# Packing the softmax row sums of eight heads, spreading their reciprocal by DMA, and running attention further ahead of an FFN

## The chip, the cores and the metric

The kernel runs on one core of one Trainium2 chip. The metric is the time of one execution on the device in microseconds (us). A single-core program can be compared run with run. All timed runs quoted as medians here are in the fast state (two probes that ran once have an unknown state, and only the durations of single instructions are read from them).

Five engines matter: TensorE (PE, matmuls), VectorE (DVE), ScalarE (ACT), GpSimd (POOL) and SyncE (SP). SP does no arithmetic here; its instruction queue issues DMAs. POOL's queue issues the DMAs that load and convert q, k, v and the weights.

## The reference

Sliding-window attention with a linear bias (ALiBi), then a gated FFN over all tokens:

```python
# q, k, v: (8 batches, 8 heads, 576 tokens, 64)
scores = q @ k.T / 8 + slope[h] * -(i - j)      # where 0 <= i - j < 128, else -1e9
attn   = softmax(scores)
x      = (attn @ v)  as (8*576, 512) tokens
out    = (gelu(x @ w_gate) * (x @ w_val)) @ w_out    # 512 -> 1536 -> 512
```

## The kernel before

Tokens are processed in nine groups of 512 for the FFN, and in eight batches of 576 for attention. A *stage* of the main loop is one group: a gate phase (`gate_val`, twelve blocks of eight matmuls) and an output phase (`out_half`, eight halves of six matmuls). The attention of the next batch is interleaved with the output phase: scores, exponential on ACT, mask on DVE, then `values` for each of four pairs of heads.

```python
    def transposes_dma(b):                      # issued by SP: ten DMA transposes per batch
        for nm, dst, off in (("ksb", kT[b % 2], 64), ("qsb", qT[b % 2], 0)):
            for j in range(5):
                ...
                nc.sync.dma_start_transpose(out=dst[:, :, off + 128 * j:...], in_=slabs[nm, b][0:sz, j, :])

    def values(b, c):                           # c: a pair of heads, i: the head in it
        ...
        for what in (0, 1):                     # 0: values, 1: row sums, with `ones` as weights
            for j in range(5):
                ...
                        w = vb[...] if what == 0 else ones          # 128 x 64
                        nc.tensor.matmul(out=ps[64 * i:64 * i + 64, base + a:base + e],
                                         lhsT=w, rhs=P[:, i, col:col + e - a], ...)
        r = r_pool.tile([128, S], FP32, name="r")
        nc.vector.reciprocal(r[:, 0:QS], z[:, 0:QS])
        nc.vector.tensor_tensor(out=xT[:, c, t0:t0 + QS], in0=x[:, 0:QS], in1=r[:, 0:QS], op=ALU.mult)
        nc.vector.reciprocal(r[:, QS:S], y[:, 256:512])
        nc.vector.tensor_tensor(out=xT[:, c, t0 + QS:t0 + S], in0=y[:, 0:256], in1=r[:, QS:S], op=ALU.mult)

    for g in range(NG):                         # the stages
        b = g + 1
        if 1 < b < B:
            load_qk(b); load_v(b)
        for f in range(NF):
            gate_val(g, f)
            if b < B and f == 0:
                transposes_dma(b)
        if b < B:
            scores0(b, 0); scores1(b, 0); out_half(g, 0); scores2(b, 0); out_half(g, 1)
            scores1(b, 1); out_half(g, 2); scores2(b, 1); values(b, 0); out_half(g, 3)
            ...                                 # and so on to values(b, 3), out_half(g, 7)
```

With 64 columns of ones as weights, the sum of a row arrives already copied to the 64 partitions where its head's values lie, so that the product needs no rearranging. The price is that each sum is inverted 64 times over.

The softmax here doesn't subtract the row's maximum and nothing guards it: scores larger than these inputs give would overflow.

## Time and profile before

| | before |
|---|---|
| time, median | 460.14 us (459.24 to 460.41, three runs) |
| span of the profiled execution | 457.4 us |
| first gate block with all its data | 48.3 us |
| a stage with attention | 51 us (the first two), 47.5 us (the later ones) |
| a stage without attention (the last two) | 31.1 us |

The head of the profile's page, busy time of each engine:

```profile
span 457.4 us, 6209 instructions
PE 377.6 (83%) x2424; PEld 179.0 (39%) x2424; DVE 283.7 (62%) x332; ACT 173.0 (38%) x314; POOL 110.3 (24%) x138
...
PE 54%; DVE 38%; ACT 3%; POOL 2%; issue 2%; POOLq 0%
```

The last line is the chain of work that ended last, followed back from the end, as shares of the span by engine. No engine is busy all the time, so the average tells little; a stage has to be cut into its phases. Busy time of each engine in the gate phase and in the output phase of one stage (start and end in us, length, then busy us and number of instructions per engine, the granted PE clock; the two last columns, of the DMA engines, are not used here):

```profile
core 0: us, PE busy (x) PEld busy (x) DVE busy (x) ACT busy (x) POOL busy (x), PEclk, DMA share, GB/s
246.90:267.10 20.20, 20.18 (x95) 9.03 (x95) 9.67 (x13) 8.50 (x14) 5.95 (x8) 1.00 0.81 98
267.10:294.40 27.30, 20.49 (x188) 10.32 (x188) 23.84 (x26) 11.46 (x23) 6.64 (x8) 0.94 0.74 78
```

The gate phase is PE alone, 20.2 us without a gap. In the output phase DVE is busy for 23.8 of 27.3 us and PE for 20.5. The chain of waits inside that phase (start, length, what), followed back from the end, says which of the two decides:

```profile
280.50 2.08 DVE r L203
...
283.09 1.67 DVE r L206
...
291.80 2.08 DVE r L203
...
294.44 0.59 PE ps L219 x2
```

Half of the chain in these 27.3 us is reciprocals (13.3 us, seven of them). In the whole kernel they cost 124.7 us, by the groups of instructions (line, engine, operation, shapes, count, then busy us in all, mean ns of one, idle time ahead):

```profile
L203 DVE RECIPROCAL r<-ps 128x320 f32<-128x320 f32 x32 | 68.8, 2150 | 0.0
L206 DVE RECIPROCAL r<-ps 128x256 f32<-128x256 f32 x32 | 55.9, 1747 | 0.0
```

SP's own queue is nearly empty. In order of time, one stage:

```profile
272.17 19.79 SPq L241 DMA_DIRECT2D out_dram<-osb  x4
292.06 6.53 SPq L127 DMA_TRANSPOSE kT<-ksb  x5
298.64 7.27 SPq L127 DMA_TRANSPOSE qT<-qsb  x5
```

Four output stores, each issued when its data is ready, then ten transposes at 1.3 us apart.

### The profile page before, as it was taken

What the parts mean: (1) busy time and instruction counts of PE and PEld (TensorE: products, weight loads), DVE (VectorE), ACT (ScalarE), POOL (GpSimd) and SP (SyncE); (2) the same over time, 40 slices, a digit from 0 to 9 for tenths busy, and PEclk for the clock granted to TensorE, in tenths of its full rate; (3) what the DMA queues carried; (4) which work ended last, traced back from release to release, by engine and by line L of the source; (5) the groups of instructions that cost most, each with busy time, mean ns of one, the idle gap of its engine ahead of it and who ended that gap; (6) DMA issues with size and microseconds to landing.
All of it is one profiled execution on the core that took longest, in us unless ns stands there. A gap on an engine that the chain in (4) does not pass through costs nothing.

```text
span 457.4 us, 6209 instructions
## 1 busy us (share of the span) xinstructions
PE 377.6 (83%) x2424; PEld 179.0 (39%) x2424; DVE 283.7 (62%) x332; ACT 173.0 (38%) x314; POOL 110.3 (24%) x138
## 2 busy tenths in 40 slices
PE   0483799669995899689968997699949995999995
PEld 0352344424442344334434443344424452344442
DVE  0579436973499346974598449944995399541430
ACT  1641237223650337233633364236514560331321
POOL 8947429122403070123303150300000000000000
PEclk9996799869997899889997999899989998899999
DMA  9999999894919592095909290940124011001002
GB/s 96 110 203 154 180 155 170 92 122 70 90 47 90 112 96 55 26 126 75 104 37 131 60 125 24 125 78 1 47 69 82 0 47 47 0 0 74 19 2 92
DMA packets 157998, 36.99 MB, mean 81 GB/s; under 512 B 147728, under 2 KB 153360, under 8 KB 157968
## 3 DMA queue, kind: packets, MB, share of 16 engines
q0 software_dynamic: 118288, 18.88, 56.4%
q1 hardware_dynamic: 39680, 17.71, 16.3%
q8 instruction: 19, 0.31, 0.3%
q14 instruction: 11, 0.09, 0.1%
HBM read 37.75 MB, written 9.44 MB: 103 GB/s over the span
## 4 chain that ended last, share of the span: by engine, by line
PE 54%; DVE 38%; ACT 3%; POOL 2%; issue 2%; POOLq 0%
PE ps L219 41%; DVE r L203 15%; PE ps L234 11%; DVE r L206 10%; DVE P L145 6%; DVE xT L204 3%; ACT P L142 3%; PE ps L135 2%; DVE xT L207 2%; POOL qsb L81 1%; DVE osb L105 1%; POOL ksb L81 1%; ACT emask L264 1%; DVE qT L105 0%; DVE emask L267 0%
## 5 line engine op out<-in xcount | busy, mean ns | idle before, releaser
L224 DVE TENSOR_TENSOR hT<-ps,gelu 128x512 bf16<-128x512 f32 x108 | 74.7, 692 | 112.4 <-PE ps L219 105.3
L219 PE MATMUL ps<-xT,wg 128*128 128x512 bf16 x432 | 117.8, 393 | 23.8 <-DVE xT L207 13.0
L219 PE MATMUL ps<-xT,wv 128*128 128x512 bf16 x432 | 114.4, 388 | 0.0
L234 PE MATMUL ps<-wo,hT 128*128 128x512 bf16 x432 | 109.9, 398 | 1.7 <-ACT osb L107 1.7
L223 ACT ACTIVATE gelu<-ps 128x512 bf16<-128x512 f32 x108 | 64.0, 597 | 120.9 <-PE ps L219 120.8
L142 ACT ACTIVATE P<-ps 128x512 bf16<-128x512 f32 (+2 forms) x160 | 73.7, 542 | 21.6 <-PE ps L135 21.6
L219 PEld LDWEIGHTS <-wv 128*128 128x128 bf16 x432 | 42.9, 99 | 76.9 <-issue 28.3
L203 DVE RECIPROCAL r<-ps 128x320 f32<-128x320 f32 x32 | 68.8, 2150 | 0.0
L219 PEld LDWEIGHTS <-wg 128*128 128x128 bf16 x432 | 43.8, 102 | 58.2 <-issue 11.5
L145 DVE TENSOR_TENSOR P<-P,emask 128x1024 bf16<-128x1024 bf16 x64 | 45.5, 721 | 26.2 <-ACT P L142 26.1
L234 PEld LDWEIGHTS <-hT 128*128 128x128 bf16 x432 | 39.5, 101 | 54.2 <-issue 17.0
L90 POOL DMA_DIRECT2D vb<-in_v_dram x40 | 34.1, 869 | 92.9 <-PE ps L197 92.1
L206 DVE RECIPROCAL r<-ps 128x256 f32<-128x256 f32 x32 | 55.9, 1747 | 0.0
L197 PE MATMUL ps<-P,vb 128*64 128x128 bf16 (+2 forms) x384 | 26.1, 282 | 32.4 <-DVE P L145 32.4
L81 POOL DMA_DIRECT2D qsb<-in_q_dram x40 | 33.8, 870 | 71.3 <-DMA qT<-qsb 64.9
L107 ACT COPY osb<-ps 128x512 f32<-128x512 f32 x18 | 10.6, 586 | 99.6 <-PE ps L234 99.6
L81 POOL DMA_DIRECT2D ksb<-in_k_dram x40 | 33.8, 887 | 17.1 <-DMA wo<-in_moe_w_out_dram 10.2
L197 PEld LDWEIGHTS <-vb 128*64 128x64 bf16 x384 | 18.7, 127 | 40.2 <-issue 38.8
L135 PE MATMUL ps<-qT,kT 64*128 64x256 bf16 (+2 forms) x320 | 27.3, 272 | 5.8 <-DVE qT L105 5.6
L197 PE MATMUL ps<-P,ones 128*64 128x128 bf16 (+2 forms) x384 | 25.8, 278 | 0.3
L135 PEld LDWEIGHTS <-kT 64*128 64x128 bf16 x320 | 10.6, 98 | 28.7 <-issue 26.6
L197 PEld LDWEIGHTS <-ones 128*64 128x64 bf16 x384 | 20.1, 130 | 1.2 <-issue 1.1
(32 smaller groups left out, 92.9 us busy)
## 6 DMA issues: line engine op xcount, KB each, us to landing
out_dram<-osb SPq DMA_DIRECT2D x36, 256.0 KB, 2.0
qsb<-in_q_dram POOLq DMA_DIRECT2D x32, 128.0 KB, 4.3
ksb<-in_k_dram POOLq DMA_DIRECT2D x32, 128.0 KB, 4.5
vb<-in_v_dram POOLq DMA_DIRECT2D x32, 128.0 KB, 4.5
wg<-in_moe_w_gate_dram POOLq DMA_DIRECT2D x4, 384.0 KB, 10.7
wv<-in_moe_w_val_dram POOLq DMA_DIRECT2D x4, 384.0 KB, 11.9
wo<-in_moe_w_out_dram POOLq DMA_DIRECT2D x1, 1536.0 KB, 17.2
kT<-ksb SPq DMA_TRANSPOSE x35, 3.2
```

What stands on the lines that cost most here:

```text
L81: nc.gpsimd.dma_start(out=t[0:sz, j, :].rearrange("p (h d) -> p h d", h=H), in_=src[b][:, 128 * j:128 * j + sz, :].rearrange("h p d -> p h ...
L90: nc.gpsimd.dma_start(out=t[lo:128, j, :].rearrange("p (h d) -> p h d", h=H), in_=v[b][:, 128 * j - 64 + lo:128 * j + 64, :].rearrange("h ...
L135: nc.tensor.matmul(out=ps[:, col:col + NQ[j]], lhsT=kT[b % 2][lo:lo + 64, c, 128 * j:128 * j + 128], rhs=qT[b % 2][lo:lo + 64, c, Q0[j]:Q0 ...
L142: nc.scalar.activation(out=dst, in_=src, func=AF.Exp, scale=0.125)
L145: nc.vector.tensor_tensor(out=dst, in0=dst, in1=m, op=ALU.mult)
L197: nc.tensor.matmul(out=ps[64 * i:64 * i + 64, base + a:base + e], lhsT=w, rhs=P[:, i, col:col + e - a], start=first, stop=last, skip_group ...
L203: nc.vector.reciprocal(r[:, 0:QS], z[:, 0:QS])
L206: nc.vector.reciprocal(r[:, QS:S], y[:, 256:512])
L219: nc.tensor.matmul(out=ps, lhsT=w[:, c, 128 * f:128 * (f + 1)], rhs=xT[:, c, t0:t0 + 512], start=(c == 0), stop=(c == 3))
L223: nc.scalar.activation(out=gl, in_=pg, func=AF.Gelu)
L224: nc.vector.tensor_tensor(out=hid[g][:, f, :], in0=pv, in1=gl, op=ALU.mult)
L234: nc.tensor.matmul(out=po, lhsT=hid[g][:, f, 128 * t:128 * (t + 1)], rhs=wo[:, f, :], start=(f == 0), stop=(f == NF - 1))
```

## The change

The intent: DVE inverts each row sum 16 times over and not 64 times, a quarter of the reciprocals. All eight heads' sums of a batch are packed into 128 rows (16 equal rows per head), one pair of reciprocals serves the batch, and 32 small DMAs spread it to the 64 partitions of each head. The spreading takes time, so attention moves further ahead: the scores of batch g+2 run in the output phase of group g, and the values of batch g+1 in its gate phase, where DVE has room.

```diff
@@ the sums and their reciprocals, once per batch
+    def sums(b):
+        ps = [bank(), bank()]
+        for j in range(5):
+            for s, a, e, col in pieces(j):
+                for i in (0, 1):
+                    for c in range(4):
+                        nc.tensor.matmul(
+                            out=ps[s][32 * c:32 * c + 32, a - QS * s:e - QS * s],
+                            lhsT=ones[:, i, :],                 # 128 x 32, ones in half of the columns
+                            rhs=probs[b, c - c % 2][:, c % 2, i, col:col + e - a], ...)
+        r = r_pool.tile([128, S], FP32, name="r")
+        nc.vector.reciprocal(r[:, 0:QS], ps[0][:, 0:QS])
+        nc.vector.reciprocal(r[:, QS:S], ps[1][:, 0:S - QS])
+        rb = r_pool.tile([128, 4, S], FP32, name="rb")
+        recip[b] = rb
+        for c in range(4):
+            for i in (0, 1):
+                row = 32 * c + 16 * i
+                for m in range(4):
+                    lo = 64 * i + 16 * m
+                    nc.sync.dma_start(out=rb[lo:lo + 16, c, :], in_=r[row:row + 16, :])
@@ values: the ones matmuls and the reciprocals are gone
-        nc.vector.reciprocal(r[:, 0:QS], z[:, 0:QS])
...
+            nc.vector.tensor_tensor(
+                out=xT[:, c, b * S + lo:b * S + hi], in0=ps[s][:, 0:hi - lo],
+                in1=recip[b][:, c, lo:hi], op=ALU.mult)
@@ the start: both batches 0 and 1 get their scores before the first gate block
+    transposes_dma(1)
+    for st in scores(0): st()
+    sums(0)
+    ...                            # scores(1) in two halves, values(0, 0..3) between and after
+    sums(1)
@@ the stages
     for g in range(NG):
+        if g + 2 < B:
+            load_qk(g + 2)
+            transposes_dma(g + 2)
         for f in range(NF):
             gate_val(g, f)
+            if g + 1 < B and f in (4, 6, 8, 10):
+                values(g + 1, f // 2 - 2)
+        b = g + 2
         if b < B:
+            load_v(b)
+            for u, st in enumerate(scores(b)):
+                st()
+                if u < 7:
+                    out_half(g, u)
+            sums(b)
+            out_half(g, 7)
```

Cut from the diff: the pools (the q/k slab goes from two buffers to one, the probabilities from two to three, the reciprocals from two to one), the output copies of most groups go to DVE alone, and the loads of batch 1's q and k move ahead of the weights.

More of the change, by code (lines that the diff above doesn't have):

```diff
@@ L48 @@
     consts = ctx.enter_context(tc.tile_pool(name="consts", bufs=1))
-    slab = ctx.enter_context(tc.tile_pool(name="slab", bufs=2))
-    p_pool = ctx.enter_context(tc.tile_pool(name="pp", bufs=2))
-    r_pool = ctx.enter_context(tc.tile_pool(name="rp", bufs=2))
+    slab = ctx.enter_context(tc.tile_pool(name="slab", bufs=1))
+    p_pool = ctx.enter_context(tc.tile_pool(name="pp", bufs=3))
+    r_pool = ctx.enter_context(tc.tile_pool(name="rp", bufs=1))
     h_pool = ctx.enter_context(tc.tile_pool(name="hp", bufs=2))
@@ L65 @@
     ident = consts.tile([128, 128], BF16, name="ident")
-    ones = consts.tile([128, 64], BF16, name="ones")
+    ones = consts.tile([128, 2, 32], BF16, name="ones")
     emask = consts.tile([128, H, 256], BF16, name="emask")
@@ L177, in scores2, with pieces @@
         mask(P[:, :, 512:1088], emask2[:, 2 * c:2 * c + 2, :])
+    def pieces(j):
+        a, e = Q0[j], Q0[j] + NQ[j]
+        if a < QS:
+            yield 0, a, min(e, QS), PCOL[j]
+        if e > QS:
+            yield 1, max(a, QS), e, PCOL[j] + max(a, QS) - a
+    recip = {}
+    def sums(b):
[7 more added lines that the diff above has]
+                            lhsT=ones[:, i, :],
+                            rhs=probs[b, c - c % 2][:, c % 2, i, col:col + e - a],
+                            start=(i == 0 and j == 2 * s), stop=(i == 1 and j == 2 * s + 2),
+                            skip_group_check=True)
+        r = r_pool.tile([128, S], FP32, name="r")
[9 more added lines that the diff above has]
+                    nc.sync.dma_start(out=rb[lo:lo + 16, c, :], in_=r[row:row + 16, :])
@@ L179, in values @@
     def values(b, c):
         P = probs[b, c - c % 2][:, c % 2]
-        x, y, z = bank(), bank(), bank()
-        for what in (0, 1):
-            for j in range(5):
-                for (a, e, ps, base) in (
-                        (Q0[j], min(Q0[j] + NQ[j], QS), (x, z)[what], 0),
-                        (max(Q0[j], QS), Q0[j] + NQ[j], y, 256 * what - QS)):
-                    if e <= a:
-                        continue
-                    first = (j == 0) if ps is not y else (j == 2 and what == 0)
-                    last = (j == 2) if ps is not y else (j == 4 and what == 1)
-                    for i in (0, 1):
-                        col = PCOL[j] + a - Q0[j]
-                        w = (vb[b % 2][:, j, 64 * (2 * c + i):64 * (2 * c + i) + 64]
-                             if what == 0 else ones)
-                        nc.tensor.matmul(
-                            out=ps[64 * i:64 * i + 64, base + a:base + e],
-                            lhsT=w, rhs=P[:, i, col:col + e - a],
-                            start=first, stop=last, skip_group_check=True)
@@ L201, in values @@
-        r = r_pool.tile([128, S], FP32, name="r")
-        t0 = b * S
-        nc.vector.reciprocal(r[:, 0:QS], z[:, 0:QS])
-        nc.vector.tensor_tensor(out=xT[:, c, t0:t0 + QS], in0=x[:, 0:QS],
-                                in1=r[:, 0:QS], op=ALU.mult)
-        nc.vector.reciprocal(r[:, QS:S], y[:, 256:512])
-        nc.vector.tensor_tensor(out=xT[:, c, t0 + QS:t0 + S], in0=y[:, 0:256],
-                                in1=r[:, QS:S], op=ALU.mult)
+        ps = [bank(), bank()]
+        for j in range(5):
+            for s, a, e, col in pieces(j):
+                for i in (0, 1):
+                    h = 2 * c + i
+                    nc.tensor.matmul(
+                        out=ps[s][64 * i:64 * i + 64, a - QS * s:e - QS * s],
+                        lhsT=vb[b % 2][:, j, 64 * h:64 * h + 64],
+                        rhs=P[:, i, col:col + e - a],
+                        start=(j == 2 * s), stop=(j == 2 * s + 2), skip_group_check=True)
@@ L210 @@
+        for s, (lo, hi) in enumerate(((0, QS), (QS, S))):
+            nc.vector.tensor_tensor(
+                out=xT[:, c, b * S + lo:b * S + hi], in0=ps[s][:, 0:hi - lo],
+                in1=recip[b][:, c, lo:hi], op=ALU.mult)
     hid = {}
@@ L238, in out_half @@
             osb = o_pool.tile([128, DM], FP32, name="osb")
-            evac(osb, po)
+            if g < B - 2:
+                nc.vector.tensor_copy(out=osb, in_=po)
+            else:
+                evac(osb, po)
             r0 = 512 * g + 128 * t
@@ L260 @@
         nc.vector.memset(vb[i][0:64, 0, :], 0.0)
-    nc.vector.memset(ones, 1.0)
+    nc.vector.memset(ones, 0.0)
+    for i in range(2):
+        nc.vector.memset(ones[:, i, 16 * i:16 * i + 16], 1.0)
     for h in range(H):
@@ L269, with scores @@
     step = DFF // 4
+    load_qk(1)
     for s in range(4):
         load_w(step * s, step * (s + 1))
-    load_qk(1)
     load_v(1)
     nc.gpsimd.dma_start(out=wo, in_=moe_w_out.rearrange("(c p) f -> p c f", p=128))
-    for c in range(4):
-        if c % 2 == 0:
-            for m in (c, c + 1):
-                transposes(0, m)
-                transposes(0, 4 + m)
-            scores0(0, c)
-        scores1(0, c)
-        scores2(0, c)
-        if c:
-            values(0, c - 1)
-    values(0, 3)
+    def scores(b):
+        for c in range(4):
+            if c % 2 == 0:
+                yield lambda c=c: (scores0(b, c), scores1(b, c))
+            else:
+                yield lambda c=c: scores1(b, c)
+            yield lambda c=c: scores2(b, c)
+    for i in (0, 1, 2, 3):
+        transposes(0, i)
+        transposes(0, 4 + i)
+    transposes_dma(1)
+    for st in scores(0):
+        st()
+    sums(0)
+    first = list(scores(1))
+    for st in first[0:4]:
+        st()
+    for c in range(2):
+        values(0, c)
+    for st in first[4:8]:
+        st()
+    for c in range(2, 4):
+        values(0, c)
+    sums(1)
     for g in range(NG):
-        b = g + 1
-        if 1 < b < B:
-            load_qk(b)
-            load_v(b)
+        if g + 2 < B:
+            load_qk(g + 2)
+            transposes_dma(g + 2)
         for f in range(NF):
             gate_val(g, f)
-            if b < B and f == 0:
-                transposes_dma(b)
+            if g + 1 < B and f in (4, 6, 8, 10):
+                values(g + 1, f // 2 - 2)
+        b = g + 2
         if b < B:
-            scores0(b, 0)
-            scores1(b, 0)
-            out_half(g, 0)
-            scores2(b, 0)
-            out_half(g, 1)
-            scores1(b, 1)
-            out_half(g, 2)
-            scores2(b, 1)
-            values(b, 0)
-            out_half(g, 3)
-            scores0(b, 2)
-            scores1(b, 2)
-            out_half(g, 4)
-            scores2(b, 2)
-            values(b, 1)
-            scores1(b, 3)
-            out_half(g, 5)
-            scores2(b, 3)
-            values(b, 2)
-            out_half(g, 6)
-            values(b, 3)
+            load_v(b)
+            for u, st in enumerate(scores(b)):
+                st()
+                if u < 7:
+                    out_half(g, u)
+            sums(b)
             out_half(g, 7)
```

## The prediction

> **What bounds it now.** In steady state one stage takes 47.5 us (chain of waits: 246.9 to 294.4): a gate phase of 20.2 us, PE alone, and an attention-and-output phase of about 27.2 us. There the chain runs through DVE: per batch four pairs of reciprocals (2.08 + 1.68 us each, 15 us), muls 3.7 us, masks 5.8 us (64 of 721 ns over 8 batches), an output copy. In that phase (busy-time windows, 267.2 to 294.4) DVE is busy 23.8 us and PE 20.4; PE stands idle up to 3.8 us at once, waiting for a mask, and its clock then falls to half for about 3 us. First gate starts about 48 us.
>
> **What the change does.** Reciprocals per batch: 15.6 us -> one pair, 3.9 us (off DVE: 11.7 us). Muls (3.7 us) move under the gate phase, where DVE has room (12 x 0.69 + 3.7 = 12 of 23 us). Output copies all go to DVE: +1.3 us. Row sums: still 48 matmuls per batch, now in four column groups instead of two; before 4 x 0.56 us, now about 1.7 us (estimate). The Trainium skill, "TensorEngine Tiling (Array Packing)", Tiling Modes, gives four independent tiles for 128x32. Small gain. PE work alone would allow a stage of about 41 us (20.7 gate + 2.4 values + 10.4 output + 3.5 scores + 1.7 sums + 2 waiting for the last mask).
>
> **What it adds.** 32 DMAs per batch on SP's queue, between the reciprocals and the ten DMA transposes of the next batch. In the trace an SP copy issue takes 332 ns plus about 0.1 us to the next; a transpose issues every 1.3 us, whether 128 or 64 rows, so I expect no discount for small copies. 32 x 0.42 = 13.4 us, plus 13 us of transposes, plus 2.4 us to landing. [...]
>
> Counted from the end of the sums: reciprocals +3.2, copies +13.4, last store +0.4, transposes +13, landing +2.4 = 32 us. But PE finishes the last output half, gate phase and values after about 24.5 us, and the scores need all those transposes. So PE waits about 7 us, its clock halves, and the output phase (9.1 output + 3.5 scores + 2 cold clock + 2 last mask + 1.7 sums) takes about 18 us. Stage: about 50 us, six times, instead of the 47.5 to 51 of before: the DVE gain is turned into a wait for SP's queue.
>
> **Start.** Both transposes and copies run on saturated DMA (9 tenths until 90 us in the slices; transposes there landed after 7 to 11 us), the values of batch 0 wait for copies queued after transposes of batch 1. First gate at about 60 to 66 us instead of 48, but holding batch 1's scores; stage 0 ends about 110 to 117.
>
> **Sum.** 113 + 5 x 49.5 + 34.5 (stage 6, no scores) + 62.2 (two stages without attention, 31.1 each) + 4.8 + 2.7 (time over span) = 465 us. Range 435 to 484. Faster by over 2%: 0.30; within: 0.30; slower: 0.40.
>
> **What would show it.** Reciprocals: 16 instructions, some 31 us in all. SP timeline: 32 copies in about 13 us, then transposes. PE: idle before the first score of each stage, released by a qT transpose, about 7 us, with half clock after. Muls inside the gate phase without waiting.
>
> **What would make it wrong.** If a 16-row copy issues in under 0.2 us, transposes land before the gate phase ends, a stage is 41 to 44 us and the kernel 410 to 435. If copies land late (DMA contention), DVE blocks on the muls and it is slower than 480. The start is the other uncertain term (10 us either way).

## The result, and the profile after

The kernel takes 524.14 us (522.81 to 524.61, four runs), against 460.27 us (459.24 to 461.43, four runs). The ratio is 1.138, with a 95% interval of 1.135 to 1.142: slower by 14%. Ratios are computed as the mean time of one kernel's fast runs over that of the other's fast runs of the same rounds, so they are not quite the ratio of the medians quoted. From the head of the profile's page:

```profile
span 522.0 us, 6526 instructions
PE 365.5 (70%) x2384; PEld 164.8 (32%) x2424; DVE 197.8 (38%) x298; ACT 164.3 (31%) x300; POOL 110.3 (21%) x138
...
PE 46%; SPq 32%; DMA 10%; issue 5%; DVE 3%; POOL 2%; ACT 1%; DVEq 0%; POOLq 0%
```

The last line is again the chain that ended last. DVE lost 86 us of work, as intended, and fell from 38% of the chain to 3%. In its place stands SPq, the issuing queue of SP, with 32%; it did not appear in the chain before. One stage, from the busy times (columns as before; now in three stretches):

```profile
...
306.40:330.10 23.70, 23.59 (x143) 10.73 (x143) 12.45 (x20) 7.39 (x13) 0.00 (x0) 1.00 0.22 50
330.10:344.60 14.50, 0.00 (x0) 0.00 (x0) 1.42 (x3) 1.06 (x1) 0.00 (x0) 0.69 0.42 101
344.60:363.50 18.90, 16.65 (x134) 6.80 (x138) 9.28 (x12) 10.64 (x21) 12.58 (x15) 0.88 1.59 137
```

The gate phase with the values in it is full, as planned. The output phase has shrunk from 27.3 to 18.9 us, as planned. Between them lie 14.5 us in which PE does nothing, and the stage is 57.1 us long instead of 47.5. The waits tell what PE and DVE wait for (engine, line, releaser, us in all, times, longest):

```profile
PE ps L135 <- DMA qT<-qsb: 112.0, 7, 25.9
...
DVE xT L227 <- DMA rb<-r: 41.8, 19, 4.8
```

(Two lines of the list of waits.) The first scores of a stage wait for the last transposes of q: once at the start (25.9 us) and six times in the stages. The second line is DVE waiting for the copies themselves before it can multiply (`xT`); whether that costs time is taken up below. SP's queue in the same stage shows where those transposes were:

```profile
308.58 20.75 SPq L212 DMA_DIRECT2D rb<-r  x32
329.43 0.53 SPq L265 DMA_DIRECT2D out_dram<-osb  x1
330.07 6.46 SPq L127 DMA_TRANSPOSE kT<-ksb  x5
336.58 6.79 SPq L127 DMA_TRANSPOSE qT<-qsb  x5
```

The 32 copies are issued first, one every 0.65 us, and the transposes come after them, because that is their order in the program. The chain of this stage shows only the second half of this:

```profile
328.26 1.85 PE ps L240 x8
330.11 1.21 SPq L127
...
342.19 2.31 DMA qT<-qsb
...
344.64 0.82 PE ps L135 x8
```

Ahead of the transposes the chain goes on with PE and not with the copies. The gate phase ended at 330.11 and the copies and the store at 330.0, so two paths end together there, and the chain, which follows inferred releases, could go on with only one. In a later stage (420 to 444 us) it goes through the copies. Such a tie is a reason to read the queue itself, and to test.

The groups of the reciprocals, which answer to those of before:

```profile
L203 DVE RECIPROCAL r<-ps 128x320 f32<-128x320 f32 x8 | 17.3, 2157 | 5.7 <-PE ps L196 5.7
L204 DVE RECIPROCAL r<-ps 128x256 f32<-128x256 f32 x8 | 13.6, 1696 | 0.0
```

And the copies in the page's list of DMA issues (count, KB each, median us from issue to landing):

```profile
rb<-r SPq DMA_DIRECT2D x256, 36.0 KB, 2.0
```

The reciprocals fell from 124.7 to 30.9 us. The copies land 2.0 us after issue (median), so they are not slow as transfers.

### The profile page after: what moved, and what is told of

It is laid out like the page before. It is cut to its first block, busy times and chain, and to the rows that moved or that the text cites. A ratio compares the mean times of both kernels' runs of the same rounds, so it can differ in the third digit from the quotient of the medians.

```text
span 522.0 us, 6526 instructions
## 1 busy us (share of the span) xinstructions
PE 365.5 (70%) x2384; PEld 164.8 (32%) x2424; DVE 197.8 (38%) x298; ACT 164.3 (31%) x300; POOL 110.3 (21%) x138
## 3 DMA queue, kind: packets, MB, share of 16 engines
q1 hardware_dynamic: 47872, 27.16, 20.8%
## 4 chain that ended last, share of the span: by engine, by line
PE 46%; SPq 32%; DMA 10%; issue 5%; DVE 3%; POOL 2%; ACT 1%; DVEq 0%; POOLq 0%
PE ps L240 20%; PE ps L255 19%; SPq L127 16%; SPq L212 15%; DMA qT<-qsb 5%; PE ps L135 4%; DMA rb<-r 4%; DMA ksb<-in_k_dram 2%; POOL qsb L81 2%; PE ps L221 1%; DVE r L204 1%; PE ps L196 1%; DVE P L145 1%; PE ps L116 1%; ACT P L142 1%
## 5 line engine op out<-in xcount | busy, mean ns | idle before, releaser
L240 PE MATMUL ps<-xT,wg 128*128 128x512 bf16 x414 | 111.6, 383 | 7.0 <-DVE xT L227 5.7
L135 PE MATMUL ps<-qT,kT 64*128 64x256 bf16 (+2 forms) x320 | 33.1, 301 | 113.9 <-DMA qT<-qsb 112.0
L245 DVE TENSOR_TENSOR hT<-ps,gelu 128x512 bf16<-128x512 f32 x108 | 74.2, 688 | 81.5 <-PE ps L240 81.4
L240 PEld LDWEIGHTS <-wg 128*128 128x128 bf16 x432 | 40.1, 98 | 50.1 <-issue 2.4
L227 DVE TENSOR_TENSOR xT<-ps,rb 128x320 bf16<-128x320 f32 x64 | 26.2, 452 | 47.0 <-DMA rb<-r 41.8
L196 PE MATMUL ps<-P,ones 128*32 128x128 bf16 (+2 forms) x384 | 13.4, 270 | 16.6 <-DVE P L145 16.6
L221 PE MATMUL ps<-P,vb 128*64 128x128 bf16 (+2 forms) x384 | 22.2, 256 | 0.0
L221 PEld LDWEIGHTS <-vb 128*64 128x64 bf16 x384 | 15.6, 115 | 12.6 <-issue 12.6
L203 DVE RECIPROCAL r<-ps 128x320 f32<-128x320 f32 x8 | 17.3, 2157 | 5.7 <-PE ps L196 5.7
L261 DVE COPY osb<-ps 128x512 f32<-128x512 f32 x24 | 16.1, 671 | 0.9 <-PE ps L255 0.8
L196 PEld LDWEIGHTS <-ones 128*32 128x32 bf16 x384 | 10.0, 107 | 20.2 <-issue 19.8
```

The lines of the kernel that those rows point to most:

```text
L135: nc.tensor.matmul(out=ps[:, col:col + NQ[j]], lhsT=kT[b % 2][lo:lo + 64, c, 128 * j:128 * j + 128], rhs=qT[b % 2][lo:lo + 64, c, Q0[j]:Q0 ...
L221: nc.tensor.matmul(out=ps[s][64 * i:64 * i + 64, a - QS * s:e - QS * s], lhsT=vb[b % 2][:, j, 64 * h:64 * h + 64], rhs=P[:, i, col:col + e ...
L240: nc.tensor.matmul(out=ps, lhsT=w[:, c, 128 * f:128 * (f + 1)], rhs=xT[:, c, t0:t0 + 512], start=(c == 0), stop=(c == 3))
L245: nc.vector.tensor_tensor(out=hid[g][:, f, :], in0=pv, in1=gl, op=ALU.mult)
```

## The experiments

The theory (A): the copies occupy SP's queue for 21 us per batch, ahead of transposes that the next scores need, and that order costs the stage its 14.5 us. The rivals: (B) the copies load the DMA engines with their bytes or landings, wherever they stand in the queue; (C) the packing or the schedule itself is the loss. The kernel before took 460.5 to 460.7 us (medians of seven runs) in the rounds of these experiments. "Stage" below is the mean distance between the first scores of successive batches, from batch 2 to batch 7: 48.2 us before, 56.8 us after.

### tr_first: only the order on SP's queue

```diff
-            transposes_dma(g + 2)          # top of stage g, behind the copies of batch g+1
+            load_qk(g + 3)                 # top of stage g
...
             load_v(b)
+            transposes_dma(b + 1)          # output phase of stage g, ahead of the copies of batch g+2
             for u, st in enumerate(scores(b)):
```

(and the first such pair ahead of `sums(1)`). The instruction order of PE, DVE and ACT was compared with that of the changed kernel and is the same; only SP's and POOL's queues differ. POOL's differs because the loads of q and k move one stage earlier too. These loads were not what the transposes waited for: for the stage shown above, the changed kernel had issued the last of them at 297.2 us, with a median of 5.2 us to landing, and the transposes began at 330.07.

> Only the order on SP's queue (and of the loads that feed it) changes: the ten transposes of a batch are issued one stage earlier, ahead of the 32 copies and not behind them. PE, DVE and ACT run the same instructions in the same order. Theory A (the scores wait for SP's queue, in which 32 copies at 0.65 us stand ahead of the transposes): the wait of PE for qT vanishes, a stage falls from 57 us to about 42, the kernel from 524 to 430 to 450 us. Rival B (the copies' data or their landing loads the DMA engines, the order is nothing): copies and transposes are still all there, 510 to 525 us. Rival C (packing and running two batches ahead is itself the loss): stays over 500 us.

Measured: 431.80 us (430.30 to 432.28), ratio to before 0.937 (0.935 to 0.940); stage 40.7 us. The copies take as long as they did, but PE no longer waits in the stages for what stands behind them. SP's queue over one stage, in order of time, and from the list of waits the same two lines (PE's only remaining wait for qT is the one at the start):

```profile
231.09 6.45 SPq L127 DMA_TRANSPOSE kT<-ksb  x5
237.58 6.47 SPq L127 DMA_TRANSPOSE qT<-qsb  x5
...
249.40 20.76 SPq L212 DMA_DIRECT2D rb<-r  x32
```

```profile
DVE xT L227 <- DMA rb<-r: 55.2, 22, 5.8
...
PE ps L135 <- DMA qT<-qsb: 25.9, 1, 25.9
```

This is theory A. Rival B falls: the same copies and the same bytes are all there. Rival C falls too: the same packing and schedule, in the same order on the three computing engines, is 6% faster than the kernel before. A further rival, that DVE is held up by copies that land late, falls as well: DVE waits longer for them here (55.2 us) than in the changed kernel (41.8 us), and the kernel is 92 us faster. The order of two things on one queue was worth these 92 us.

### half_copies: half the copies, the same bytes

```diff
-                            out=ps[s][32 * c:32 * c + 32, ...], lhsT=ones[:, i, :],
+                            out=ps[i][s][32 * c:32 * c + 32, ...], lhsT=ones,     # own banks for each i
...
-                for m in range(4):
-                    lo = 64 * i + 16 * m
-                    nc.sync.dma_start(out=rb[lo:lo + 16, c, :], in_=r[row:row + 16, :])
+                for m in range(2):
+                    lo = 64 * i + 32 * m
+                    nc.sync.dma_start(out=rb[lo:lo + 32, c, :], in_=r[32 * c:32 * c + 32, i, :])
```

> Sums of the two heads of a pair go to separate banks, 32 rows each: 16 copies of 32 rows instead of 32 of 16 rows, the same bytes, with two more reciprocals per batch (3.9 us of DVE). Theory A: 16 x 0.65 = 10.4 us less on SP's queue per batch, of which up to 3.9 us may be given back by the reciprocals ahead: a stage of 47 to 51 us, the kernel 455 to 490 us. Rival B (bytes): no change, 520 to 530.

Measured: 465.32 us (two runs, 464.15 and 466.49), ratio 1.011; stage 48.7 us. That is 8.1 us less per stage for 16 copies fewer, within what A said. So another dose of the same cause moves the time with it. SP's queue in one stage:

```profile
265.58 12.37 SPq L212 DMA_DIRECT2D rb<-r  x16
```

### small_copies: the same copies, a ninth of the bytes

```diff
-                    nc.sync.dma_start(out=rb[lo:lo + 16, c, :], in_=r[row:row + 16, :])
+                    nc.sync.dma_start(out=rb[lo:lo + 16, c, 0:64], in_=r[row:row + 16, 0:64])
```

The products read the 64 columns over and over, so the result is wrong.

> The same 32 copies of 16 rows, but of 64 columns instead of 576: a ninth of the bytes, the same count. The result is wrong on purpose (one sum in nine is used for all). Theory A (issue slots): no change, 515 to 527 us, copies still 0.6 us or more apart. Rival B (bytes on the DMA engines): the stages lose most of their 15 us wait, below 470 us.

Measured: 508.74 us (two runs, 506.84 and 510.64), ratio 1.105; stage 54.6 us. The copies take as long as with nine times the bytes (SP's queue, one stage):

```profile
295.95 20.59 SPq L212 DMA_DIRECT2D rb<-r  x32
```

The kernel is 15 us below the changed one, a little outside what A said. Much of that is a side effect of the edit: copies of the first 64 columns need only the first of the two reciprocals. The first copy came 18.9 us after the stage's first score here (277.1 to 295.95) and 20.2 us in the changed kernel (288.4 to 308.6), and over the five stages between batches 2 and 7 the means are 18.8 and 20.8 us, so 2.0 of the 2.2 us per stage. (That the second reciprocal is the reason is argued, not tested.) Bytes are not what costs 14.5 us: the copies and the store behind them, from the first copy to the first transpose, take 21.3 us instead of 21.6.

### bcast_pe: no copies at all

```diff
-        rb = r_pool.tile([128, 4, S], FP32, name="rb")
-        ... 32 dma_start
+        r = r_pool.tile([128, S], BF16, name="r")              # written by the reciprocals
...  in values(b, c):
+        pr = [bank(), bank()]
+        rb = r_pool.tile([128, S], BF16, name="rb")
+            nc.tensor.matmul(out=pr[s][:, 0:hi - lo], lhsT=sel[:, c, :], rhs=recip[b][:, lo:hi], ...)
+            nc.scalar.copy(out=rb[:, lo:hi], in_=pr[s][:, 0:hi - lo])
```

`sel` has a one where row 32c + 16i meets the 64 columns of head (c, i).

> No copies at all: the packed reciprocals are spread by two matmuls per pair with a 0/1 selection matrix, read out by ACT (bfloat16), all else as in the changed kernel. Theory A: the transposes land 16 us after the sums, inside the gate phase; a stage of 42 to 43 us; the first gate starts at about 67 us instead of 78; the kernel at 420 to 435 us. Rival C (packing and running two batches ahead is itself the loss): over 490 us.

Measured: 419.44 us (418.67 to 419.58), ratio 0.911 (0.908 to 0.913); correct; stage 41.4 us in every stage, the first gate block at 68.0 us. The gate block is 1 us later than expected; stage and time lie just under their ranges (42 to 43 and 420 to 435 us). The spreading costs PE 64 matmuls of 128x320 or 128x256, and the granted clock is 0.998 on average (0.895 in the changed kernel). The edit also gives the reciprocals two buffers and bfloat16, which was not tested apart. A stage in two stretches, from the busy times (columns as before):

```profile
...
233.50:258.00 24.50, 24.50 (x153) 11.51 (x151) 13.44 (x22) 10.06 (x21) 5.90 (x8) 1.00 0.58 80
258.00:274.80 16.80, 15.14 (x137) 6.29 (x137) 9.92 (x13) 11.72 (x22) 6.68 (x9) 1.00 1.32 124
```

PE is busy for 39.6 of 41.3 us, so PE is now the bound. This version beats both kernels.

### ahead_only: the schedule without the packing

The new schedule with the old `values` of the kernel before (ones matmuls and reciprocals for each pair of heads), and without `sums` and copies.

> The new schedule (scores two batches ahead, values in the gate phase) with the old sums: every pair of heads has its own ones matmuls and reciprocals, no copies. Tells what the schedule is worth without the packing. Per stage DVE then has 36 us (15.6 reciprocals, 3.7 muls, 8.3 gate products, 5.8 masks, 2.7 output copies) against some 43 us of PE; at the four values DVE needs 6.2 us where PE needs 4.2. If the schedule alone brings the gain of bcast_pe: stages of 43 to 46 us, the kernel 425 to 450 us. If the packed reciprocal is what is needed: stages stay at 47 us or more, 455 us or more.

Measured: 460.90 us (459.91 to 461.44), ratio 1.001 (0.998 to 1.004): no gain. The two tests of the expectation disagree: the time is in the second range, but the stages are 44.4 us, in the first. What the stages gain is lost elsewhere. At the start the values of batch 0 stand between the scores of batch 1, DVE runs 15.6 us of reciprocals there before the first gate block, and that block gets its data only at 81.4 us (68.0 in bcast_pe). The end of the chain of waits up to there:

```profile
76.61 2.07 DVE r L211
...
79.20 1.68 DVE r L214
...
81.38 8.83 PE ps L227 x30
```

So the packed reciprocal is what makes the schedule pay: between this kernel and bcast_pe lie 41 us. The packing without the new schedule was not run.

### probe and probe2: what one issue costs

Both are the kernel before with groups of twelve DMAs between dead tiles appended on SP's queue (each ran once).

> The kernel before, with 48 copies between dead SBUF tiles appended on SP's queue, back to back, in groups of twelve: 128 rows of 2,048 B, 16 rows of 2,304 B, 16 rows of 256 B, 32 rows of 2,304 B. If the 0.63 us between copies belongs to an issue whatever it moves, all four groups show about 0.63 us from start to start. If it is the smallness or the SBUF destination that makes a copy dear, the groups differ: 0.43 us for the 128-row group as the prediction assumed for all. If bytes count, the 256 B group is the fastest.

SP's queue at the end of the run, in order of time, a group a line:

```profile
455.70 8.40 SPq L332 DMA_DIRECT2D xT<-wg  x12
464.20 7.54 SPq L336 DMA_DIRECT2D xT<-wg  x12
471.79 7.54 SPq L340 DMA_DIRECT2D xT<-wg  x12
479.37 7.55 SPq L343 DMA_DIRECT2D wv<-wg  x12
```

In this order: 128 rows of 2,048 B; 16 rows of 2,304 B; 16 rows of 256 B; 32 rows of 2,304 B. Twelve issues take 7.5 us, 0.63 us each, and neither rows nor bytes change it (the 128-row group, 0.70 us, is a little slower). A copy of 16 rows costs SP about what one of 128 rows costs.

> The kernel before, with appended groups of twelve: (1) 16-row copies on SP to one and the same place, so that each waits for the landing of the last; (2) 128-row loads from DRAM on SP, back to back; (3) 16-row copies from ACT's queue, back to back; (4) 16-row copies alternating between SP and ACT. The output stores of this kernel, each issued alone after a wait, show 332 ns, copies in a row 587 ns at 0.63 us. If the short record belongs to an issue that waited, group 1 shows about 332 ns; if it belongs to stores to DRAM or to the row count, group 1 stays at 533 to 587 ns. If a row of issues costs 0.63 us whatever its ends are, groups 2 and 3 show 0.63 us too. If the limit is SP's own queue and not one shared unit behind both, group 4 takes 0.63 us per pair; if shared, 1.26 us per pair.

One instruction on SP or ACT (line, queue, form, count, shortest/median/longest ns, first and last start):

```profile
L332 SPq DMA_DIRECT2D xT<-wg x12: 507/507/731, 454.9 to 477.0; - x12
L335 SPq DMA_DIRECT2D xT<-in_moe_w_val_dram x12: 371/431/608, 477.5 to 483.2; - x12
L339 ACTq DMA_DIRECT2D wv<-wg x12: 600/608/852, 454.4 to 461.9; - x12
```

For comparison, in the same view, the stores of the kernel before, from which the prediction took its figure, and the copies of the changed kernel:

```profile
L241 SPq DMA_DIRECT2D out_dram<-osb x36: 332/332/362, 74.9 to 453.2; - x36
```

```profile
L212 SPq DMA_DIRECT2D rb<-r x256: 507/587/1724, 48.4 to 443.7; - x128
```

A copy from one on-chip tile to another takes 507 ns of SP even when it is issued alone after a wait (L332, probe2), which is in neither range of the expectation, and 587 ns in a row. A store to DRAM issued alone takes 332 ns; behind the copies, in the changed kernel, the same store takes 0.53 us. Loads from DRAM in a row take 431 ns (12 in 6.09 us, 0.5 us each). In tr_first three stores stand in a row behind the transposes: 1.50 us for the three, 0.5 us each. So two things make the copies dearer than the store that the prediction took its figure from: both ends are on-chip (507 instead of 332 ns alone, 0.63 instead of 0.5 us in a row), and they come in a row. The numbers of rows differ too, but the first probe showed that they hardly matter. ACT's queue is not cheaper (608 ns). The fourth group, which should have shown whether SP and ACT hold each other up, failed: ACT's queue ran ahead of SP's and the two did not alternate. The trace still shows a part of it: ACT's copies (454.4 to 470.5 us) overlapped in time with SP's first group, and SP's lone issues took 507 ns then as they did afterwards. What two full rows do to each other stays open.

### early_gate: filling the wait at the start

bcast_pe, with the values of batch 0 and the first six gate blocks moved ahead of the scores of batch 1:

```diff
     sums(0)
-    ...                            # scores(1) and values(0, .) interleaved
+    for c in range(4):
+        values(0, c)
+    for f in range(6):
+        gate_val(0, f)
+    for st in scores(1):
+        st()
     sums(1)
```

(and `values(1, .)` at gate blocks 8 to 11 of the first group).

> bcast_pe with the start rearranged: the values of batch 0 and the first six gate blocks of group 0 run in the 25.7 us in which PE waits for the first qT transposes. Theory: that wait is only filled, not shortened; six blocks of 1.73 us are hidden, less two more table loads of ACT: 406 to 414 us against 419. If the start is bound by the loads and not by PE's order, the blocks wait for weights and the gain is under 3 us.

Measured: 413.72 us (413.16 to 414.54), ratio to before 0.899 (0.897 to 0.901), correct: the fastest kernel here. The gain of 5.7 us is in the expected range, at its small end. The six blocks fit (37.5 to 48.7 us), the wait for qT remains, and some of what it hid is paid back by the clock. PE in order of time:

```profile
56.57 3.77 PE L136 MATMUL ps<-qT,kT 64*128 64x128 bf16 x29 [7.87 <-DMA qT<-qsb]
...
68.35 1.89 PE L241 MATMUL ps<-xT,wg 128*128 128x512 bf16 x4
...
72.77 1.03 PE L241 MATMUL ps<-xT,wv 128*128 128x512 bf16 x4
```

After 7.9 us of rest and some sparse work, four gate matmuls take 1.89 us instead of 1.03 until about 72 us.

## Why the prediction was wrong

The direction it thought most likely (slower, at 0.40) and the mechanism were right; the size was not: 465 us predicted, range to 484, 524 measured. The direction owes something to luck, since 465 us is within 2% of the kernel before. The step that failed is the term "32 x 0.42 = 13.4 us", and with it the sentence "I expect no discount for small copies". There was no discount, but there was a surcharge that it had not looked for. One stage, from the end of the sums (305.2 us) to the end of the next (362.2 us):

| term | predicted, us | measured, us |
|---|---|---|
| reciprocals | 3.2 | 3.4 (to 308.6) |
| 32 copies on SP's queue | 13.4 | 20.8 |
| last store | 0.4 | 0.7 |
| transposes and their landing | 15.4 | 14.4 (330.07 to 344.50) |
| output phase with scores and sums | 18 | 17.6 |
| stage | about 50 | 57.0 |

- **What bounded the kernel before**: right. Moving the reciprocals out of the output phase (ahead_only) brings the stage to 44.4 us, and packing them as well (bcast_pe) to 41.4; the prediction put PE's work alone at about 41.
- **The wait for SP's queue**: right in kind. PE waits for qT transposes behind the copies, and tr_first, which changes that order and nothing on PE, DVE and ACT, removes the wait and 92 us. It said about 7 us per stage; measured 14.5, and the 7.5 us between are the 7.4 us by which the copies were mis-sized.
- **Where the figure came from**: one output store, issued alone to DRAM, 332 ns plus 0.1 us. Nothing in the trace of before showed copies between on-chip tiles, or issues of that kind in a row. The honest range for the term was 0.33 us to well over 0.5, and only the low end had been considered as a risk ("under 0.2 us"). The probes: 507 ns alone, 0.63 us in a row.
- **The start**: predicted 60 to 66 us for the first gate block, measured 78.4. It is the same term for the larger part: the first 32 copies took 24.2 us there (seen apart in tr_first, whose start is the same; 48.4 to 72.6), 10.8 us more than 13.4. The last of them also landed 5.3 us after its issue there, and not after about 2.0 us as in the stages.
- **The sum**: stage 0 ends at 135.5 us, where the next gate block starts, and not at 113: 22.5 us. Five stages of 57.1 us (135.5 to 420.9) and not 49.5: 38 us. The end and the time over the span take 1.2 us off. Together 59 us, which is what is missing from 465 to 524.
- **The end**: stages 6 to 8 and the tail predicted 101.5 us, measured 101.1 (from 420.9).
- **Sums in four column groups**: predicted 1.7 us per batch, a small gain. The Trainium skill, "TensorEngine Tiling (Array Packing)", section Tiling Modes, names four independent column tiles for 128x32; in the trace 45 of the 48 sums take 1.10 us, against 0.63 to 0.66 us for twelve before (at the full clock), so the trace agrees that they overlap more.
- **The clock**: PE's clock falls while it waits. The Trainium skill, "TensorE: Matmul & The Clock Gate", section "What's actually happening", gives half clock after an idle window of about 3.4 us. The trace agrees: in the stage shown the granted clock goes to half 5.4 us into the wait (335.5) and back to full at 349.1, 4.5 us after its end. It averages 0.69 over the 14.5 us wait and 0.88 over the phase after it, and 0.895 over the kernel, against 0.998 in bcast_pe.
- **Landing**: the Trainium skill, "DMA: Bandwidth & Descriptors", section "Anatomy of one DMA — SWDGE (gpsimd) path", gives a fixed cost of about 2.0 us for a DMA issued from GpSimd. The copies are issued from SP, and in the trace they also land after 2.0 us (median). These 2 us were not the problem; they overlap. What does not overlap is the issue on one queue. The prediction expected the products in the gate phase without waiting, and named products held up by late copies as what would take it over 480 us. DVE did wait for copies, 41.8 us in all, but PE waited for a product only 5.7 us in the whole kernel, all of it before the first gate block had its data. In the stages it reached PE once, for 0.7 us (at 447.6 us).

What stays open: why a row of issues is dearer than one alone, whether SP and ACT hold each other up when both issue in a row, and what the packing gives without the new schedule.

## What to carry to other kernels

A queue that only issues DMAs is an engine with a serial cost per instruction, so count its instructions per stage and ask what stands behind them: here 32 copies of 36 KB, cheap as transfers, held up ten transposes that the next phase needed. Before adding something to an in-order queue, put first what others wait for, even a stage early; that alone turned a loss of 14% into a gain of 6%. And when sizing a new instruction from a trace, take the duration from the same form in the same situation (both ends, alone or in a row), or carry the doubt into the range.

## What the Trainium skill lacked or had wrong

- "DMA: Bandwidth & Descriptors", section "Anatomy of one DMA", splits the fixed cost and gives about 50 ns for the sequencer's dispatch, on the path issued from GpSimd; no page has the serial cost of an issue on SP measured on this chip (this page's part on trn3 B0 has sequencer cycles per instruction for "previous generations", which it does not name). The runs show 332 ns for a store to DRAM alone (three in a row 0.5 us each), 431 ns for loads from DRAM in a row, 507 ns for a copy between on-chip tiles alone and 587 ns (0.63 us apart) in a row; in the first probe it is 0.63 us with 16 or 32 rows, of 256 or 2,304 B, and 0.70 us with 128.
- The same page, section "Rules for kernel authors", says that many small transfers should be made one large one because those under 64 KB pay mostly overhead. That agrees in direction, but the cost here was not in the transfer: with a ninth of the bytes the 32 copies held SP's queue for 20.6 us instead of 20.8.
- The page has no issue cost for a DMA transpose that was measured on this chip (with the same exception); the traces show 1.2 us of SP each, 1.3 us apart, for 128 and for 64 rows alike.
